# Emitting the five engine programs into the main body in place of a block

## The chip, the cores and the metric

The kernel runs on one core of one Trainium2 chip. The metric is device microseconds of one execution. Each kernel was executed several times. The profile gives a second number, the span: from the first to the last instruction of the kernel's own program. For most runs below, time and span of the same execution are both listed, so that their difference can be taken. That difference will matter: I call it the tail. It is what the timed stretch holds outside the kernel's own instructions; part of it may lie before the first of them, so only differences between tails are put down to the end of the program. Spans are listed to 0.1 us, so one tail is good to about 0.05 us.

The profile's names of the engines: PE is TensorE (PEld its weight loads), DVE VectorE, ACT ScalarE, POOL GpSimd, SP SyncE. A semaphore is a counter that the program has one engine or a transfer raise and another engine wait for (at the end of the kernel before, SyncE's wait for the output transfer's is recorded with 0.9 us). A drain is a sequencer's instruction of the barrier; those at the end of the kernel before end just after the last work of their engine (VectorE's at 364.96 us, its last copy at 364.91; ScalarE's at 364.94 and 364.90; TensorE's at 364.51 and 364.43).

## The reference

Two independent attention decode steps, A and B, with their own inputs and one query position. The last 4096 positions of a 16384 position cache are attended, and the two outputs are concatenated (shortened):

```python
def _A_ref(x, k_cache, v_cache, wq, wo):        # _B_ref is the same
    B, Sq, D = x.shape                           # 2, 1, 576
    Hq, Dh = 32, 128
    Hkv, Sk = k_cache.shape[1], k_cache.shape[2] # 16, 16384
    W = min(4096, max(256, Sk // 4))
    rep = Hq // Hkv
    q = (x @ wq).reshape(B, Sq, Hq, Dh).transpose(0, 2, 1, 3)
    k = jnp.repeat(k_cache[:, :, Sk - W:, :], rep, axis=1)
    v = jnp.repeat(v_cache[:, :, Sk - W:, :], rep, axis=1)
    p = _softmax(jnp.einsum("bhqd,bhkd->bhqk", q, k) * (Dh ** -0.5))
    o = jnp.einsum("bhqk,bhkd->bhqd", p, v)
    return o.transpose(0, 2, 1, 3).reshape(B, Sq, Hq * Dh) @ wo
# returns concatenate([A, B], axis=-1): (2, 1, 1152) bf16
```

## The kernel before

A small static scheduler first records every operation for each of five engines, with the operations that it depends on. Then `emit` writes one engine's list out, with semaphore waits between engines. Loads of K, V and the weights are issued by SyncE in one long stream. The change touches only the frame around these lists.

```python
    es = ExitStack()
    with es:
        block = es.enter_context(nc.Block())
        # ... (tensors, semaphores, all operations recorded; cut)

        def emit(eng_name, engine):
            for op in S.ops[eng_name]:
                # ... (waits for op.deps; cut)
                last = op.fn(engine)
                if op.dma is None:
                    last.then_inc(ev[eng_name], 1)

        @block.sync
        def _(e):
            emit("sp", e)
            e.wait_ge(out_sem, dma_count[out_sem])   # the outputs have landed

        @block.tensor
        def _(e):
            emit("pe", e)

        @block.vector
        def _(e):
            emit("dve", e)

        @block.scalar
        def _(e):
            emit("act", e)

        @block.gpsimd
        def _(e):
            emit("pool", e)
```

The program that this builds has a main body (constants, one all-engine barrier, five branches), one body for each engine, and an end body with a second all-engine barrier. The trace of this kernel records one branch in all, SyncE's to the end body, which carries the wait for the output. A barrier is recorded like this: each engine drains, and the drains of the four other than GpSimd count up one semaphore (at the end of this kernel the last of them, SyncE's, at 366.343 us). GpSimd waits for that semaphore (366.375) and then counts up a release semaphore (366.454), for which the other four wait (366.495 to 366.558).

## Time and profile before

| | before |
|---|---|
| time, three runs | 368.84, 368.87, 368.89 us |
| span of the profiled execution | 366.6 us |
| HBM rate over the span | 418 GB/s |
| first load issued | 0.81 us into the span |
| last engine's end minus end of SyncE's wait for the output | 0.35 us |

The first load issued, from the timeline (start, duration, engine, line, operation, tile):

```profile
0.81 0.41 SPq L180 DMA_DIRECT2D ring<-in_A_wq_dram  x1
```

The profile page of the kernel before, cut: the span; busy time of each engine, its share of the span and its instructions; then two rows of 40 equal slices of the span (busy tenths of the DMA engines, and what they moved); the bytes; and the chain of waits that ended last, by engine.

```profile
span 366.6 us, 3694 instructions
PE 271.8 (74%) x1700; PEld 101.0 (28%) x1435; DVE 185.9 (51%) x189; ACT 34.3 (9%) x114; POOL 14.1 (4%) x53
...
DMA  8999999999999999999999999999999999999994
GB/s 322 447 408 427 429 429 423 432 426 427 429 431 427 427 427 426 426 427 428 424 428 431 427 426 429 431 426 429 429 419 429 429 429 429 421 428 429 425 415 183
...
HBM read 153.10 MB, written 0.00 MB: 418 GB/s over the span
...
DMA 82%; DVE 13%; PE 4%; SPq 0%; issue 0%
```

Loads run from the first slice to the last, between them at 400 to 450 GB/s, and 82% of the chain is waiting for them. On that chain, nothing that the change touches lies between slice 1 and slice 40.

The last pieces of that chain in order of time (start, duration, what):

```profile
324.29 36.06 DMA ring<-in_B_v_cache_dram
...
362.93 1.38 PE pj L683 x14
364.31 0.17 PE pj L673 x2
364.48 0.43 DVE out_sb L693
```

The chain ends with VectorE's copy at 364.9 us. It ends with a computing instruction, so it doesn't show the output transfer and the barrier behind it. Those are seen by asking for the source line to which the block's closing instructions belong (engine and instruction, count, duration in ns, start of the first and of the last in us; a small q marks a sequencer's instruction):

```profile
L94 POOLq EVENT_SEMAPHORE  x2: 17/17/17, 366.4 to 366.5; - x2
L94 POOLq DRAIN  x1: 394/394/394, 285.2 to 285.2; - x1
...
L94 SPq COMPARE_BRANCH  x1: 33/33/33, 366.2 to 366.2; - x1
L94 SPq DRAIN  x1: 7/7/7, 366.3 to 366.3; - x1
L94 SPq EVENT_SEMAPHORE  x1: 17/17/17, 366.5 to 366.5; - x1
...
L94 PEldq EVENT_SEMAPHORE  x1: 51/51/51, 366.5 to 366.5; - x1
```

GpSimd had drained at 285 us already and waits there. SyncE's wait for the output stands at 366.2 us (recorded as a compare-and-branch). Everything after it is the branch to the end body and the barrier. The same instructions from the trace's records, in us from the start of the span, to the nanosecond:

```
366.174  33 ns  SyncE    COMPARE_BRANCH   waits for the output's semaphore
366.343   7 ns  SyncE    DRAIN            counts itself in
366.375  17 ns  GpSimd   EVENT_SEMAPHORE  all four are in
366.454  17 ns  GpSimd   EVENT_SEMAPHORE  releases the four
366.495  17 ns  SyncE    EVENT_SEMAPHORE  (ScalarE 366.499, VectorE 366.506)
366.507  51 ns  TensorE  EVENT_SEMAPHORE  the last instruction, ends 366.558
```

### The profile page before, as it was taken

The page shows a single profiled execution, that of the slowest core. Times are in us where ns is not written, and L with a number is a line of the kernel's source. Part 1 is how long each engine was busy: PE and PEld are TensorE (multiplying, and loading weights), DVE is VectorE, ACT ScalarE, POOL GpSimd, SP SyncE. Part 2 cuts the span into 40 slices and gives each one's busy share as a digit, 9 for nine tenths or more (in the row PEclk, how much of TensorE's full clock was granted, in tenths as well). Part 3 has the DMA queues.
Part 4 walks back from the last instruction along what each step waited for, and adds up shares of the span by engine and source line. Part 5 has one row for each costly group of instructions (what it writes and reads, how often), then busy time and mean ns, then how long its engine had stood idle before and what let it go on. Part 6 is the DMA issues. An engine that isn't in the chain of part 4 may idle for free.

```text
span 366.6 us, 3694 instructions
## 1 busy us (share of the span) xinstructions
PE 271.8 (74%) x1700; PEld 101.0 (28%) x1435; DVE 185.9 (51%) x189; ACT 34.3 (9%) x114; POOL 14.1 (4%) x53
## 2 busy tenths in 40 slices
PE   0635975987679788567968876794996677498797
PEld 0311112122214322132314321151223222143554
DVE  3104997967543674435744584407745476233100
ACT  1011002002000110002000020001200030002100
POOL 5010000000000000000000000000000000000000
PEclk9976897698985889895895998867798989958958
DMA  8999999999999999999999999999999999999994
GB/s 322 447 408 427 429 429 423 432 426 427 429 431 427 427 427 426 426 427 428 424 428 431 427 426 429 431 426 429 429 419 429 429 429 429 421 428 429 425 415 183
DMA packets 11264, 153.34 MB, mean 418 GB/s; under 512 B 1256, under 2 KB 1392, under 8 KB 2032
## 3 DMA queue, kind: packets, MB, share of 16 engines
q1 hardware_dynamic: 11236, 153.10, 98.6%
q8 instruction: 12, 0.20, 0.2%
q14 instruction: 4, 0.03, 0.0%
q10 hardware_dynamic: 12, 0.01, 0.0%
HBM read 153.10 MB, written 0.00 MB: 418 GB/s over the span
## 4 chain that ended last, share of the span: by engine, by line
DMA 82%; DVE 13%; PE 4%; SPq 0%; issue 0%
DMA ring<-in_B_k_cache_dram 41%; DMA ring<-in_A_k_cache_dram 28%; DVE xt L437 12%; DMA ring<-in_B_v_cache_dram 10%; DMA ring<-in_A_wq_dram 4%; PE ot L274 1%; PE st L461 1%; PE st L381 1%; PE pj L683 0%; PE st L395 0%; SPq L373 0%; PE st L594 0%; SPq L368 0%; DVE out_sb L693 0%; DVE ssum L536 0%
## 5 line engine op out<-in xcount | busy, mean ns | idle before, releaser
L437 DVE STREAM_TRANSPOSE xt<-ring 128x2048 f32<-128x2048 f32 x64 | 144.5, 2287 | 91.3 <-DMA ring<-in_A_k_cache_dram 46.7
L461 PE MATMUL st<-xt,zq 128*128 128x512 bf16 x256 | 115.6, 452 | 62.6 <-DVE xt L437 62.5
L381 PE MATMUL st<-xt,zq 128*128 128x512 bf16 x256 | 115.6, 451 | 0.0
L461 PEld LDWEIGHTS st<-xt,zq 128*128 128x128 bf16 x256 | 28.4, 111 | 158.8 <-DVE xt L437 82.7
L585 PE MATMUL ot<-ring,pT 128*32 128x512 bf16 x448 | 55.1, 395 | 0.7 <-ACT oE L610 0.7
L585 PEld LDWEIGHTS ot<-ring,pT 128*32 128x32 bf16 x448 | 20.5, 100 | 33.8 <-issue 15.4
L620 PEld LDWEIGHTS tb<-selv,oE 128*128 128x128 f32 x112 | 21.1, 280 | 5.8 <-issue 4.0
L620 PE MATMUL tb<-selv,oE 128*128 128x16 f32 x112 | 19.8, 324 | 0.8 <-ACT oE L610 0.8
L424 POOL TENSOR_TENSOR zq<-qs,bmask 128x64 bf16<-128x64 bf16 x32 | 9.2, 292 | 270.5 <-PE st L381 177.9
L639 DVE TENSOR_TENSOR oA<-tb,cmask 128x256 bf16<-128x256 f32 x7 | 3.0, 425 | 29.1 <-PE tb L620 29.1
L610 ACT ACTIVATE oE<-ot,rsb 128x512 f32<-128x512 f32 x14 | 9.6, 685 | 84.2 <-PE ot L585 84.2
L512 ACT ACTIVATE pR<-st,bias_sb 128x256 bf16<-128x256 f32 x32 | 15.9, 545 | 0.3
L471 DVE TENSOR_REDUCE mx<-st 128x2 f32<-128x512 f32 x16 | 10.0, 664 | 3.0 <-PE tb L651 3.0
L683 PE MATMUL pj<-wob,oP 128*2 128x288 bf16 x126 | 10.9, 324 | 0.3 <-ACT oP L655 0.3
L531 DVE STREAM_TRANSPOSE pT<-pR 128x512 bf16<-128x512 bf16 x16 | 10.4, 685 | 0.0
L501 PE MATMUL tb<-ones_f,nMrep 1*128 1x1 f32 x32 | 5.6, 276 | 6.0 <-DVE nMrep L495 6.0
L505 ACT ACTIVATE bias_sb<-tb 128x2 f32<-128x2 f32 x8 | 1.4, 172 | 89.1 <-PE tb L501 89.1
L255 PE MATMUL tb<-ident_b,xt 2*128 2x2 bf16 x36 | 2.3, 194 | 9.9 <-DVE xt L222 9.9
L655 ACT ACTIVATE oP<-tb 128x16 bf16<-128x16 f32 x8 | 1.5, 191 | 86.8 <-PE tb L651 86.8
L594 PEld LDWEIGHTS st<-pT,ring 128*128 128x128 bf16 x256 | 7.4, 102 | 5.1 <-DMA ring<-in_B_v_cache_dram 4.9
L594 PE MATMUL st<-pT,ring 128*128 128x16 bf16 x256 | 7.7, 173 | 0.5 <-DMA ring<-in_B_v_cache_dram 0.4
L631 DVE TENSOR_TENSOR oA<-st,cmr 128x64 bf16<-128x64 f32 x4 | 0.9, 225 | 13.7 <-PE st L594 13.7
(67 smaller groups left out, 92.7 us busy)
## 6 DMA issues: line engine op xcount, KB each, us to landing
ring<-in_A_k_cache_dram SPq DMA_DIRECT2D x16, 2048.0 KB, 33.2
ring<-in_A_v_cache_dram SPq DMA_DIRECT2D x16, 2048.0 KB, 35.8
ring<-in_B_k_cache_dram SPq DMA_DIRECT2D x16, 2048.0 KB, 37.1
ring<-in_B_v_cache_dram SPq DMA_DIRECT2D x15, 2048.0 KB, 36.9
ring<-in_A_wq_dram SPq DMA_DIRECT2D x1, 4608.0 KB, 13.8
ring<-in_B_wq_dram SPq DMA_DIRECT2D x1, 4608.0 KB, 24.3
wob<-in_A_wo_dram SPq DMA_DIRECT2D x4, 1152.0 KB, 33.5
wob<-in_B_wo_dram SPq DMA_DIRECT2D x3, 1152.0 KB, 30.8
```

The lines of the kernel that those rows point to most:

```text
L381: return e.add_instruction(mybir.InstMatmult(name=nc.get_next_instruction_name(), engine=mybir.EngineType.PE, ins=[e.lower_ap(mv), e.lower ...
L424: return e.tensor_tensor(dst, src, msk, ALU.mult)
L437: Xop[(t, jb)] = S.add("dve", lambda e: e.transpose(xt[:, n % NXT, :].bitcast(FP32), ring[:, r, jb * HW_:(jb + 1) * HW_].bitcast(FP32)), d ...
L461: last = e.matmul(st[bk][:, 0:512], wt, mv, start=first, stop=True, skip_group_check=True)
L471: mxs = [S.add("dve", lambda e, jb=jb: e.tensor_reduce(mx[:, jb, :], st[jb][:, :].rearrange("p (x t) -> p t x", t=2), AX.X, ALU.max), [Sop ...
L512: last = e.activation(pR[:, jb, :].rearrange("p (x t) -> p t x", t=2)[:, t, :], st[jb][:, :].rearrange("p (x t) -> p t x", t=2)[:, t, :], ...
L531: chain[(G, "pT%d" % jb)] = S.add("dve", lambda e, jb=jb: e.transpose(pT[:, v, 512 * jb:512 * jb + 512].rearrange("p (w j q) -> p j w q", ...
L585: last = e.matmul(OTB[32 * c:32 * c + 32, :], pT[:, v, col:col + 32], ring[:, r, j * 128:(j + 4) * 128], start=(j % 32 == 0), stop=(j % 32 ...
L594: last = e.matmul(OL[m % 2][:, 0:16], ring[:, r, j * 128:(j + 1) * 128], pT[:, v, col:col + 16], start=(j == 0), stop=(j == KR - 1))
L610: evac_op[(G, pr)] = S.add("act", lambda e: e.activation(oE[:, pr, :], OTB[:, :], ACTF.Copy, scale=rsb[:, v, pr:pr + 1]), deps, "oE%d_%d" ...
L620: last = e.matmul(bank[:, 0:16], oE[:, pr, 128 * c:128 * c + 128], selv[:, pr, c, :], start=(pr == 0 and c == 0), stop=(pr == 1 and c == 3))
L683: last = e.matmul(PJ[half], oP[:, v, j, :], wob[:, v, j, half * NH:(half + 1) * NH], start=(proj_start(G) and j == 0), stop=True, skip_gro ...
```

## The change

The intent: no branch at entry and no all-engine barrier at the end. SyncE still waits for the output.

```diff
     with es:
-        block = es.enter_context(nc.Block())
 ...
-        @block.sync
-        def _(e):
-            emit("sp", e)
-            e.wait_ge(out_sem, dma_count[out_sem])
-        @block.tensor
-        def _(e):
-            emit("pe", e)
-        (the same for vector, scalar, gpsimd)
+        emit("sp", nc.sync)
+        nc.sync.wait_ge(out_sem, dma_count[out_sem])
+        emit("pe", nc.tensor)
+        emit("dve", nc.vector)
+        emit("act", nc.scalar)
+        emit("pool", nc.gpsimd)
```

More of the change, by code (lines that the diff above doesn't have):

```diff
@@ L782, in emit @@
                     last.then_inc(ev[eng_name], 1)
-        @block.sync
-        def _(e):
-            emit("sp", e)
-            e.wait_ge(out_sem, dma_count[out_sem])
-        @block.tensor
-        def _(e):
-            emit("pe", e)
-        @block.vector
-        def _(e):
-            emit("dve", e)
-        @block.scalar
-        def _(e):
-            emit("act", e)
-        @block.gpsimd
-        def _(e):
-            emit("pool", e)
+        emit("sp", nc.sync)
[4 more added lines that the diff above has]
+        emit("pool", nc.gpsimd)
 def bass_concat_heads__sliding_block_cached__sliding_block_cached__decode_kernel(
```

## The prediction

> **What bounds the kernel now.** The DMA stream. The page of before gives 418 GB/s over a 366.6 us span, and the chain of waits that ended last is 82% DMA, 13% VectorE transposes of K, 4% TensorE.  Nothing in the middle of the program is touched by the change, so the only places that can move are the first and the last microsecond.
>
> **What the change removes at entry.** The timeline shows no branch. SyncE leaves the entry barrier at 0.724 us (a 17 ns semaphore wait) and its first load starts at 0.809 us: 68 ns after the wait ended. Two neighbouring semaphore instructions of GpSimd are 61 ns apart, which is plain issue. So the entry branch is either folded into fall-through or costs about nothing.[...] The barrier at entry (0.00 to 0.74 us) belongs to the program's start, not to the block, and stays. Gain at entry: 0 us[...].
>
> **What the change removes at the end.** After the last output transfer landed, SyncE's wait (recorded as a compare-and-branch) ran 366.174 to 366.207 us. Then come a gap of 136 ns (the branch to the end block), a 7 ns drain on SyncE at 366.343, GpSimd's gather at 366.375 and release at 366.454, and the last engine's release ended at 366.558 us, the end of the span. From the end of the wait to the end of the span that is 0.35 us, all of it serial and on the critical path: nothing else runs there. The drains of TensorE, VectorE and ScalarE (0.40 to 0.48 us) lie beside the work they drain, worth nothing.
>
> **What it adds or moves.** The wait for the output becomes a plain semaphore wait (17 ns as elsewhere in the trace). The other four engines leave the program early[...]. The time is 2.3 us above the span (368.87 against 366.56)[...].
>
> Each instruction stream keeps its order and loses two to four entries[...].
>
> **Prediction.** 368.87 - 0.35 at the end[...]: 368.45 us. Range 367.9 to 368.85. Faster by over 2%: 0.5%. Within 2%: 99%. Slower: 0.5%.
>
> **What would show each step.** In the profile after: first load still at about 0.81 us; no drain and no barrier semaphores at the end, the span ending with SyncE's wait for the output at about 366.2 us; GB/s and chain unchanged; the time minus the span still about 2.3 us.
>
> **What would make it wrong.** The time may fall by more than the span[...] (time minus span below 2.2 us), or by nothing[...] (time minus span grows to about 2.65 us).[...]

The forecast's sum came to 368.45 us: 368.87 less the 0.35 at the end, and less a second term of 0.07 us. That term stood for the four other engines ending before SyncE. It was a guess of mine, worked out from no trace.

## The result

| | before | after |
|---|---|---|
| time, median of 4 runs (range) | 368.86 us (368.82 to 368.89) | 367.33 us (367.05 to 367.79) |
| span of the profiled execution | 366.6 us | 365.9 us |
| tail of the four runs | not listed for these runs | 1.28, 1.29, 1.27, 1.25 us |

The ratio is 0.9964 (95% interval 0.995 to 0.9978). Ratios here are the mean time of one kernel's fast runs over that of the other's in the same rounds, so not quite the ratio of the medians. The means of the listed runs would give 0.9960, so the runs of before behind the 0.9964 are not just these four; by the ratio the gain is about 1.3 us, by the medians 1.5 us. By the 2% rule (a difference under 2% counts as none) the kernels are the same. The difference is nevertheless clear of noise (the interval does not reach 1), and the time fell below the predicted range of 367.9 to 368.85 us.

The page of the kernel after, the same lines:

```profile
span 365.9 us, 3683 instructions
PE 273.0 (75%) x1700; PEld 101.6 (28%) x1435; DVE 185.8 (51%) x189; ACT 34.3 (9%) x114; POOL 14.2 (4%) x53
...
DMA  8999999999999999999999999999999999999995
GB/s 323 451 410 428 430 428 422 436 424 424 430 424 430 428 430 428 421 430 429 428 424 433 428 426 424 428 426 428 430 424 425 428 430 430 424 427 426 427 414 205
...
HBM read 153.10 MB, written 0.00 MB: 418 GB/s over the span
...
DMA 81%; DVE 12%; PE 5%; ACT 1%; issue 1%; SPq 0%
```

The stream is the same. The end of the chain of waits:

```profile
332.67 30.78 DMA wob<-in_B_wo_dram
363.45 0.04 issue
363.49 0.53 PE pj L682 x6
364.02 0.17 PE pj L672 x2
364.19 0.43 DVE out_sb L692
```

The last weight load landed at 363.81 us in this execution and at 364.07 us in the one of before (read from the load's semaphore). That is 0.26 us by chance of the stream: in the 14 traces this moment lies between 363.70 and 364.24 us, whichever kernel it is. Which load's wait the chain is put down to also changes between executions, and nothing follows from it. The source line of SyncE's wait is all that is left at the end:

```profile
core 0 of [0], span 365.9 us
engine op xcount: duration ns min/median/max, first and last start us, forms
L784 SPq EVENT_SEMAPHORE  x1: 17/17/17, 365.9 to 365.9; - x1
```

From the trace's records: that wait runs 365.890 to 365.907 us, and the span ends with it. VectorE and ScalarE ended at 364.62, TensorE at 364.15, GpSimd at 287.3 us. At entry nothing changed: SyncE leaves the entry barrier at 0.725 and issues its first load at 0.810 us (before: 0.724 and 0.809):

```profile
0.81 0.42 SPq L179 DMA_DIRECT2D ring<-in_A_wq_dram  x1
```

Neither trace records a branch at entry, so this shows that the block costs nothing there, and not what a branch costs.

So the entry and the barrier's 0.35 us came out as predicted. What the span cannot show is the rest: the tail is 1.27 us where I had taken 2.3 us for before.

### The profile page after: what moved, and what is told of

It is laid out like the page before. It is cut to its first block, busy times and chain, and to the rows that moved or that the text cites. A ratio compares the mean times of both kernels' runs of the same rounds, so it can differ in the third digit from the quotient of the medians.

```text
span 365.9 us, 3683 instructions
## 1 busy us (share of the span) xinstructions
PE 273.0 (75%) x1700; PEld 101.6 (28%) x1435; DVE 185.8 (51%) x189; ACT 34.3 (9%) x114; POOL 14.2 (4%) x53
## 4 chain that ended last, share of the span: by engine, by line
DMA 81%; DVE 12%; PE 5%; ACT 1%; issue 1%; SPq 0%
DMA ring<-in_B_k_cache_dram 41%; DMA ring<-in_A_k_cache_dram 28%; DVE xt L436 11%; DMA wob<-in_B_wo_dram 8%; DMA ring<-in_A_wq_dram 4%; PE st L460 1%; PE st L380 1%; PE ot L273 1%; PE tb L619 1%; ACT pR L511 1%; PE pj L682 0%; DVE pT L530 0%; SPq L372 0%; PE tb L500 0%; DVE out_sb L692 0%
## 5 line engine op out<-in xcount | busy, mean ns | idle before, releaser
L584 PE MATMUL ot<-ring,pT 128*32 128x512 bf16 x448 | 57.2, 407 | 0.7 <-ACT oE L609 0.7
L619 PEld LDWEIGHTS tb<-selv,oE 128*128 128x128 f32 x112 | 22.1, 293 | 6.0 <-issue 4.2
L619 PE MATMUL tb<-selv,oE 128*128 128x16 f32 x112 | 21.0, 335 | 0.8 <-ACT oE L609 0.8
L682 PE MATMUL pj<-wob,oP 128*2 128x288 bf16 x126 | 10.1, 305 | 0.9 <-DMA wob<-in_B_wo_dram 0.6
L485 DVE TENSOR_REDUCE nM<-tb 1x8 f32<-1x64 f32 x16 | 2.7, 207 | 11.4 <-PE tb L476 11.4
```

Source lines behind the costliest of these rows:

```text
L584: last = e.matmul(OTB[32 * c:32 * c + 32, :], pT[:, v, col:col + 32], ring[:, r, j * 128:(j + 4) * 128], start=(j % 32 == 0), stop=(j % 32 ...
L619: last = e.matmul(bank[:, 0:16], oE[:, pr, 128 * c:128 * c + 128], selv[:, pr, c, :], start=(pr == 0 and c == 0), stop=(pr == 1 and c == 3))
L682: last = e.matmul(PJ[half], oP[:, v, j, :], wob[:, v, j, half * NH:(half + 1) * NH], start=(proj_start(G) and j == 0), stop=True, skip_gro ...
```

## The experiments

Twelve programs were run (e5 is the changed kernel again), on three chips, four to a chip, each set next to the kernel before, whose runs now list their spans too. First, this gives the tail of the kernel before: over its 23 runs the mean is 1.96 us, the range 1.80 to 2.08. So 2.3 us does not describe it; I had paired the span of one execution with the times of others. The fall of the tail from 1.96 to 1.27, 0.69 us, is what has to be explained.

The theories were guesses, set up to be told apart by the runs. Theory A: each engine's end is followed by a piece of the tail of its own (the expectations call it closing work, which is only a name: no trace records what it is), and the barrier makes all five pieces begin when SyncE's does. Theory B: it's the branch to the end body, and fetching instructions behind it. Theory C: it's chance in the loads.

| kernel | ends last | tail, us: mean (range) | ratio to before (95%) |
|---|---|---|---|
| before, 23 runs | all, by barrier | 1.96 (1.80 to 2.08) | |
| after, 9 runs | SyncE | 1.27 (1.24 to 1.29) | 0.9964, 0.9965 |
| e1 barrier in main body | all, by barrier | 1.95 (1.91 to 1.98) | 0.9996 (0.9981 to 1.0011) |
| e2 wait behind the block | SyncE; barrier 0.5 us earlier | 1.47 (1.42 to 1.61) | 0.9979 (0.9964 to 0.9994) |
| e3 all five wait | all, no barrier | 1.89 (1.82 to 1.92) | 0.9995 (0.998 to 1.001) |
| e4 GpSimd waits | GpSimd | 1.90, 1.88, 1.90 and once 2.47 | 0.999 (0.9974 to 1.0007) |
| e4 ScalarE waits | ScalarE | 1.45 (1.42 to 1.48) | 0.9973 (0.9958 to 0.9988) |
| e4 VectorE waits | VectorE | 1.40 (1.33 to 1.50) | 0.998 (0.9962 to 0.9999) |
| e4 TensorE waits | TensorE | 1.55 (1.48 to 1.62) | 0.9974 (0.9959 to 0.9989) |
| e6 all but GpSimd wait | four | 1.57 (1.52 to 1.62) | 0.997 (0.9955 to 0.9985) |
| e7 GpSimd until last copy | SyncE, GpSimd 1.24 us earlier | 1.38 (1.35 to 1.42) | 0.9968 (0.9951 to 0.9984) |
| e8 with short memset | SyncE, GpSimd 0.64 us earlier | 1.34, 1.34, 1.35 and once 1.86 | 0.9968 (0.9953 to 0.9983) |
| e9 with long memset | SyncE, GpSimd 0.17 us earlier | 1.75 (1.70 to 1.79) | 0.998 (0.9965 to 0.9995) |

All outputs are right. Spans jitter by some tenths between executions (366.2 to 367.4 us in the 23 runs of before), so the tail decides more sharply than the ratio.

### e1_barrier_in_main: the barrier without block and branch

```diff
         emit("pool", nc.gpsimd)
+        nc.all_engine_barrier()
```

> The changed kernel with the all-engine barrier put back at its end, but in the main body: no block, no branch. Theory A[...]: time minus span as before, 2.3 us, span about 366.2 to 366.7, time about 368.6 to 368.8 us. Theory B (the branch to an end block and the instruction fetch behind it make the 1.0 us outside the span): time minus span stays at 1.3 us, time about 367.6 us. Theory C (the 1.0 us is chance of the loads): time minus span anything, not near either.

Measured: tail 1.95 us, median time 368.25 us, ratio 0.9996. The barrier's instructions, by their source line in this kernel:

```profile
L789 POOLq EVENT_SEMAPHORE  x2: 17/17/17, 366.0 to 366.1; - x2
...
L789 SPq DRAIN  x1: 7/7/7, 366.0 to 366.0; - x1
L789 SPq EVENT_SEMAPHORE  x1: 17/17/17, 366.1 to 366.1; - x1
...
L789 PEldq EVENT_SEMAPHORE  x1: 51/51/51, 366.1 to 366.1; - x1
```

Theory B falls: with no branch and no end body the whole tail of before is back, and theory C with it, since four tails lie within 0.07 us. The trace also splits the 0.35 us. From the start of SyncE's wait to the start of its drain it is 56 ns here (365.929 to 365.985), where the wait is a plain semaphore instruction, and 169 ns before, where it is the compare-and-branch. So, with one trace of each, the branch costs 0.11 us more than the plain wait (169 less 56 ns) and the barrier behind it about 0.22 us (here 365.985 to 366.201, before 366.343 to 366.558).

### e2_wait_behind_block: block and barrier kept, but under the output transfer

```diff
-        block = es.enter_context(nc.Block())
 ...
+        blk = nc.Block()
+        block = blk.__enter__()
         @block.sync
         def _(e):
             emit("sp", e)
-            e.wait_ge(out_sem, dma_count[out_sem])
 ...
+        blk.__exit__(None, None, None)
+        nc.sync.wait_ge(out_sem, dma_count[out_sem])
```

> The kernel before with its block, its branches and its barrier, but SyncE's wait for the output stands behind the block: the barrier runs while the output transfer is in flight (1.2 us) and SyncE alone ends last. Theory A: time minus span 1.3 us and time as the changed kernel, 367.1 to 367.8 us, though branch and barrier are all still there. Theory B: if the branch itself costs, it now costs under the transfer too, so the time also falls; B is told apart by e1, not here. If the mere presence of a barrier in the program costs 1.0 us: time minus span 2.3 us, time about 368.5 us.

Measured: tail 1.47 us (median 1.44), median time 367.69 us, ratio 0.9979. The barrier, and then SyncE's wait, by their source lines:

```profile
L806 POOLq EVENT_SEMAPHORE  x2: 17/17/17, 365.6 to 365.6; - x2
...
L806 SPq DRAIN  x1: 155/155/155, 365.4 to 365.4; - x1
```

```profile
L807 SPq EVENT_SEMAPHORE  x1: 17/17/17, 366.2 to 366.2; - x1
```

The barrier is over at 365.7 us and SyncE's wait comes at 366.2. So a barrier that is present but runs under the transfer costs little (tail 1.47 us, against 1.27 without and 1.96 with it at the end). Of the branch this run says nothing, against what the expectation took for granted: its trace records no branch at all, since the wait that the branch carried has been moved. The tail is not quite the 1.27 us of the changed kernel, and that fits theory A: GpSimd's last instruction ended at 365.65 us, only 0.54 us ahead of SyncE. Adding GpSimd's 1.9 us (see e4) to that gives a tail of 1.36; 1.44 was measured (the median).

### e3_all_engines_wait: no barrier, but all five end together

```diff
         emit("pool", nc.gpsimd)
+        nc.tensor.wait_ge(out_sem, dma_count[out_sem])
+        nc.vector.wait_ge(out_sem, dma_count[out_sem])
+        nc.scalar.wait_ge(out_sem, dma_count[out_sem])
+        nc.gpsimd.wait_ge(out_sem, dma_count[out_sem])
```

> The changed kernel, no block and no barrier, but each of the five engines waits for the output itself before it ends. Theory A: all five start their closing work at the end of the span, so time minus span is near 2.3 us (span about 366.0, time about 368.3 us); only the 0.35 us of the barrier are saved. Theory B or a cost of the barrier's own instructions: time minus span 1.3 us, time 367.1 to 367.8 us.

Measured: tail 1.89 us; the times scattered from 367.82 to 368.72 us because the spans did (365.9 to 366.9). GpSimd's wait in its trace:

```profile
core 0 of [0], span 365.9 us
...
L792 POOLq EVENT_SEMAPHORE  x1: 17/17/17, 365.9 to 365.9; - x1
```

There is no barrier, no drain and no branch at the end here, and nearly all of the tail is back (0.62 of the 0.69 us). So nearly all of it comes from engines ending late and not from the instructions of the barrier. The size given in the expectation, 2.3 us, was still the wrongly paired one.

### e4: one engine alone waits for the output

The edit, with `gpsimd`, `scalar`, `vector` or `tensor`:

```diff
         emit("sp", nc.sync)
-        nc.sync.wait_ge(out_sem, dma_count[out_sem])
 ...
         emit("pool", nc.gpsimd)
+        nc.gpsimd.wait_ge(out_sem, dma_count[out_sem])
```

> The changed kernel, but GpSimd waits for the output in place of SyncE, which ends right after issuing the transfer. Theory A says which engine is last decides what of the closing work is exposed: if GpSimd's own closing work is longer than SyncE's, time minus span is between 1.3 and 2.3 us; if it is the same or shorter, 1.3 us or less. Theory B: 1.3 us whichever engine waits.

> The changed kernel, but ScalarE alone waits for the output. Theory A2 (GpSimd alone has the long closing work): time minus span near SyncE's 1.3 us. If every engine other than SyncE has the long closing work: 1.9 us as with GpSimd.

> The changed kernel, but VectorE alone waits for the output. Theory A2: time minus span near 1.3 us. If every engine other than SyncE has the long closing work: 1.9 us. Below 1.25 us it would be a better place for the wait than SyncE.

> The changed kernel, but TensorE alone waits for the output. Theory A2: time minus span near 1.3 us. If every engine other than SyncE has the long closing work: 1.9 us. Below 1.25 us it would be a better place for the wait than SyncE.

GpSimd's wait is the end of its kernel's span (this profiled execution is the one with the tail of 2.47 us and a late span; its other three tails are 1.88 to 1.90):

```profile
core 0 of [0], span 367.0 us
...
L788 POOLq EVENT_SEMAPHORE  x1: 17/17/17, 367.0 to 367.0; - x1
```

Measured: SyncE 1.27 (the changed kernel), VectorE 1.40, ScalarE 1.45, TensorE 1.55, GpSimd 1.90 us. The two extremes are clear (VectorE and ScalarE overlap), but the "near 1.3 us" of theory A2 (theory A with the long closing work on GpSimd alone) was met only loosely by the three in between. GpSimd last costs 0.63 us more than SyncE last, which is nearly the whole tail of the barrier. No place for the wait is better than SyncE, so none of these four beats the changed kernel.

### e5_after_again: the changed kernel beside the kernel before, with spans

No edit.

> The changed kernel once more, on one chip with the kernel before and with the span of every run listed. On this footing kernel before showed time minus span of 1.92 us (mean of seven runs), not the 2.3 us of the prediction. Theory A2 (GpSimd needs about 1.9 us from its release to the end of the timed stretch, SyncE 1.3 us; the barrier makes GpSimd start as late as SyncE): time minus span 1.25 to 1.30 us, that is 0.65 us less than before, span 0.3 us less (the barrier) give or take the loads' jitter of 0.3 us; time 0.8 to 1.1 us below before, ratio 0.997 to 0.998. If the first measurement's 1.5 us holds instead, ratio 0.996, then something in the span beyond the barrier is gained as well.

Measured: median 367.38 us, nine runs of before 368.72 us, ratio 0.9965 (0.9952 to 0.9979). Means: time 368.72 to 367.45, so 1.27 us less, of which tail 1.97 to 1.27 (0.71 us) and span 366.74 to 366.18 (0.56 us). The gain of the first measurement is repeated, somewhat above the 0.8 to 1.1 us that I expected.

### e6_all_but_gpsimd_wait: four late engines and an early GpSimd

```diff
         emit("pool", nc.gpsimd)
+        nc.tensor.wait_ge(out_sem, dma_count[out_sem])
+        nc.vector.wait_ge(out_sem, dma_count[out_sem])
+        nc.scalar.wait_ge(out_sem, dma_count[out_sem])
```

> The changed kernel with four engines (SyncE, TensorE, VectorE, ScalarE) waiting for the output and GpSimd left free to end early. If the time from an engine's end to the end of the timed stretch is each engine's own and the longest counts (SyncE 1.27, VectorE 1.40, ScalarE 1.45, TensorE 1.55, GpSimd 1.9 us): time minus span about 1.55 us. If it grows with the number of engines that come late rather than with which: about 1.8 us. If GpSimd plays no special part: 1.9 us as with all five.

Measured: 1.57 us, TensorE's own figure (1.55). Four late engines cost what the slowest of them costs alone. In this run it's the maximum over the engines that counts, not their number; and GpSimd alone carries the step from 1.57 to 1.89 us (e3). So GpSimd is not all of it: with GpSimd long gone, the other four still cost 0.30 us over SyncE alone.

### e7, e8, e9: GpSimd's end moved in steps, everything else as changed

```diff
         emit("pool", nc.gpsimd)
+        nc.gpsimd.wait_ge(ev["dve"], e_ops[(NPROB - 1, 0)].seq)          # e7, e8, e9
+        nc.gpsimd.memset(xU[...], 0.0)   # e8 only: 128x576 fp32
+        nc.gpsimd.memset(zq[...], 0.0)   # e9 only: 128x1152 fp32
```

Both tensors are no longer read at that point.

> The changed kernel, SyncE alone waits for the output, but GpSimd stays in the program until VectorE's last copy, which lies 1.2 to 1.3 us before SyncE's end, in place of ending some 78 us earlier. Rule under test: the timed stretch ends at the later of SyncE's end + 1.27 us and GpSimd's end + 1.9 us. 1.2 us of lead is more than the 0.65 us needed, so time minus span stays at 1.27 us. If GpSimd must be away for much longer for the gain: above 1.4 us.

> As the run before, and after that wait GpSimd runs one memset of 0.58 us (the duration of the same memset at the start of the program), so it ends about 0.6 us before SyncE. The rule gives the threshold: time minus span 1.27 to 1.4 us.

> As the run before, with a memset of 1.06 us in place of 0.58 us, so GpSimd ends about 0.1 to 0.2 us before SyncE. The rule gives time minus span 1.7 to 1.85 us. If GpSimd's end only matters when it is the last of all: 1.27 us. No barrier, no branch and no wait of GpSimd for the output is in this kernel.

The timeline of e9's last microseconds (start, duration, engine, line, operation; in brackets GpSimd's idle time and what ended it):

```profile
core 0 of [0], span 366.1 us
...
364.89 1.06 POOL L790 MEMSET zq<- 128x1152 f32 x1 [77.44 <-DVE out_sb L692]
364.91 0.33 SPq L696 DMA_DIRECT2D out_dram<-out_sb  x1
```

GpSimd ends at 365.94 us, 0.17 us ahead of SyncE's wait (366.11). The rule "SyncE's end + 1.27 or GpSimd's end + 1.9, whichever is later" gives 1.73; measured 1.75. With 0.64 us of lead (e8) the tail was 1.34, 1.34, 1.35 and once 1.86; with 1.24 us of lead (e7) it was 1.38. So between 0.64 and 1.24 us, more lead brings nothing: most of the gain comes from GpSimd's last microsecond. The rule is too simple, though. e7 and e8 stay 0.07 to 0.11 us above 1.27, which it doesn't give. It also falls short where a barrier closes the program: there GpSimd ends 0.09 us before the span does (366.471 of 366.558 us in before, 366.113 of 366.201 in e1), so the rule gives a tail of 1.81, and 1.96 and 1.95 were measured. It thus explains about 0.54 of the 0.69 us, and 0.15 us of it stay without a cause. The two single outliers of about 0.5 us, one here and one with GpSimd alone waiting, have no explanation.

## Why the prediction was wrong

- **"The DMA stream" bounds the kernel, and the middle doesn't move:** right. 418 GB/s and the same chain in both.
- **"Gain at entry: 0 us":** right. First load at 0.809 and 0.810 us; no branch is recorded there, so there was none to gain.
- **0.35 us at the end, "all of it serial and on the critical path":** right in the trace: the end of SyncE's wait is now the end of the span. e1 divides it into 0.11 us for the branch behind the wait and the rest for the barrier.
- **The 0.07 us for four engines ending early**: this is the step that failed. The direction was right and the size was not: it measured 0.69 us (tail 1.96 to 1.27). No trace showed a size when I gave it one, and a range all the same. Engines that end early save far more than that: e3 brings 0.62 us back without a barrier, and e4, e6 and e9 put the largest part on GpSimd.
- **"The time is 2.3 us above the span (368.87 against 366.56)":** wrong as a pairing. Times and span were not of the same execution; 23 paired runs give 1.96, and none reaches 2.1. With the true pair the forecast "time minus the span still about 2.3 us" had no basis either.
- **The range:** three times within 0.05 us made me take the kernel as steady. Later runs of before spread from 368.07 to 369.48 us. My low end of 367.9 left room for 0.97 us in all, less than the known terms below.

The known terms make 0.35 + 0.69 = 1.04 us. The measured gains are 1.5 us (first medians; 1.3 by the ratio) and 1.27 us (e5, means). The rest is in the span: the mean over all 23 runs of before is 366.73, over all 49 runs of kernels without a closing barrier at the end 366.27 us, a difference of 0.47 with a standard error of 0.08. By chip it is 0.20, 0.48 and 0.65 us, each good to 0.10 to 0.16. So the 0.12 us beyond branch and barrier are not shown to be real, nor are the 0.2 to 0.4 us in the changed kernel's own runs; the scatter of the loads is as large, and I leave that open. Also open is what each engine does in the tail: the profile holds no instruction of it. Whether GpSimd's part is long in itself or comes first in some order among the engines was not told apart. That GpSimd's late end carries the largest part is shown; the mechanism inside is only argued.

No version beat the changed kernel: its tail is the shortest of all that were tried.

## What to carry to other kernels

The timed stretch holds more than the span, and which engines end late decides how much: here it was 1.27 us with SyncE last and 1.90 with GpSimd, and the branch and all-engine barrier at the end cost 0.35 us in the span and twice that (0.69) outside it, above all because the barrier held GpSimd back. Let every engine leave as soon as its own work is done, GpSimd early (0.64 us ahead of SyncE gave a tail within 0.1 us of the shortest in three runs of four), and let SyncE alone wait for the output. Before reasoning about time minus span, take both from the same execution, and take several.
